# A third Strassen product taken as seven quarter-size products, with its right sums reloaded from DRAM

**Chip, cores, metric.** One core of a Trainium2 chip. The time is device microseconds of that core, given as the median of several executions.

## The reference, cut to what matters

```python
# attention between x (8 batches, 8 heads, 512 tokens, 64) and state (32 rows), both ways;
# concatenated tokens: 8 * (512 + 32), width 512
h = x @ w_in                                # 512 -> 2048
g = h * (1.0 / (1.0 + np.exp(-1.702 * h)))
return (g @ w_out).astype(np.float32)       # 2048 -> 512
```

The products with `w_in` are called up products here, those with `w_out` down products. All matmuls are fp32. TensorE does the matmuls and writes them to banks of the PSUM memory; VectorE does the sums. The batches go one after the other; then come the summary rows of all batches together ("sr" in the names).

## The kernel before

The product with `w_out` of batches 1 to 7 is one level of Strassen's scheme in Winograd's form: seven products P1 to P7 of halves. The weight is cut into B11, B21, B22, with the sums T1, T2, T3, T4 kept for all batches; the activations are cut into A11 to A22. Two of the seven, P6 (with T2) and P7 (with T3), are themselves done as seven products of quarters, by the function below. It needs sums of the left operand (made on VectorE in each batch) and of the right one (kept: `low2`, `low3`).

```python
def strassen_low(left, right, bank, R, at):
    b11, t3, b21, b22, t1, t2, t4 = right
    a11, a12, a21, a22, s1, s2, s4 = left
    p, u2, u3 = (pu[:, i] for i in range(3))
    o = [v[:, :P] for v in bank]                # three PSUM banks, used in turn
    ...
    product(o[0], a11, b11)                     # each product: 4 matmuls of 128 columns
    nc.scalar.copy(p, o[0])
    at(1)                                       # at(i): other work hooked in here
    product(o[1], s2, t2)
    add(u2, o[1], p)
    at(2)
    product(o[2], a12, b21)
    add(c11, o[2], p)
    at(3)
    product(o[0], a21, t3)
    add(u3, o[0], u2)
    at(4)
    product(o[1], s1, t1)                       # the bank of the second product again
    add(c22, o[1], u3)
    add(c12, o[1], u2)
    ...                                         # a22 t4, then s4 b22
```

A whole product is 2 x 8 matmuls of 256 columns. The end of a batch, in the order in which it is issued:

```python
    # P1, P2, P5 whole, P6 as seven small ones with T2, then:
    ...                                          # left sums for P7, eight VectorE operations
    for u in range(NU // 2, NU):
        s4(u)                                    # A12 made ready for P3
    tt(t01, bank(0), k2)
    hook("P6")
    product(bank(2), A_of(1, 1), T4, "P4")       # whole
    strassen_low(..., low_banks(), k3, ...)      # P7 with T3
    tt(k3, k3, k2)
    ...                                          # two outputs
    product(bank(3), A_of(0, 1), B22, "P3")      # whole
    tt(o01, bank(3), t01)
```

The hooks carry the attention and the up-product sums of the next batch; in batch 7 they carry the sums for the summary rows instead. In these traces VectorE's operations and TensorE's matmuls stand in the order in which the kernel issues them, so what is hooked in ahead of a sum delays that sum. The up products of the next batch follow directly.

Of the kernel before, what the change touches and what calls it, by code (L numbers as in the profile page):

```python
# [10 lines left out]
FP32 = mybir.dt.float32  # L11
# [3 lines left out]
ALU = mybir.AluOpType  # L15
# [5 lines left out]
def kernel(  # L21
# [30 lines left out]
    nc = tc.nc  # L52
# [27 lines left out]
    mpool = ctx.enter_context(tc.tile_pool(name="mpool", bufs=4))  # L80
    gpool = ctx.enter_context(tc.tile_pool(name="gpool", bufs=1))
    opool = ctx.enter_context(tc.tile_pool(name="opool", bufs=1))
    psA = ctx.enter_context(tc.tile_pool(name="psA", bufs=2, space=bass.MemoryType.PSUM))
    psH = ctx.enter_context(tc.tile_pool(name="psH", bufs=2, space=bass.MemoryType.PSUM))
    psO = ctx.enter_context(tc.tile_pool(name="psO", bufs=1, space=bass.MemoryType.PSUM))
# [495 lines left out]
    T3 = w_out[:, :HF, HN:]  # L581
    low2, low3 = ([low[:, 3 * i + k].rearrange("p (f n) -> p f n", f=QF) for k in range(3)] for i in range(2))

    def halves_of(t):

        return [t[:, QF * i : QF * (i + 1), P * k : P * (k + 1)] for i in range(2) for k in range(2)]

    def low_sums(t, rooms):

        b11, b12, b21, b22 = halves_of(t)  # L590
        t1, t2, t4 = rooms
        return [(T_of, v) for v in ((t1, b12, b11), (t2, b22, t1), (t4, b21, t2))]
# [40 lines left out]
        add(c12, o[0], c12)  # L633
        at(7)

    def strassen_two(key, dst, hooks):

        B11, B21, B22 = w_out[:, :HF, :HN], w_out[:, HF:, :HN], w_out[:, HF:, HN:]
        g = [G[key, u] for u in range(HF)]
        half = S // 2  # L640

        def A_of(i, k):
            return [quarters(key, (HF * k + f) // 2, S)[i][:, f % 2] for f in range(HF)]

        def hook(name):
            for fn, args in hooks.get(name, ()):
                fn(*args)

        def bank(i):
            return bank_o[i].rearrange("p (r n) -> p r n", r=2)  # L650

        def product(ps, lhs, rhs, name):
            for r in range(2):
                for f in range(HF):
                    nc.tensor.matmul(  # L655
                        ps[:, r], lhs[f][:, P * r : P * (r + 1)], rhs[:, f],
                        start=(r == 0 and f == 0), stop=(f == HF - 1), skip_group_check=True,
                    )
                hook(name + "ab"[r])

        def tt(out, x0, x1, op=ALU.add):
            nc.vector.tensor_tensor(out=out, in0=x0, in1=x1, op=op)

        def room(i):
            return later[:, i].rearrange("p (r n) -> p r n", r=2)

        def out(i, k, src):
            nc.sync.dma_start(dst(slice(2 * i, 2 * i + 2), slice(HN * k, HN * (k + 1))), src)

        def low_banks():  # L670
            h = [psH.tile([P, FC], FP32, tag="h", name=f"low_{key}") for _ in range(2)]
            return [bank_o[1], *h]


        q1, q2, q4 = (g[i][:, :, :half].rearrange("p k (h t) -> p k h t", h=2) for i in range(3))
        v1, v2, v4 = (later[:, 1 + i].rearrange("p (f t) -> p f t", f=QF) for i in range(3))
        k1 = g[3][:, :, :half]
        k2, k3, t01, o10, o01 = (room(i) for i in (0, 4, 5, 6, 7))
        z11, z12, z21, z22 = ([S2[:, QF * k + f, P * i : P * (i + 1)] for f in range(QF)] for i in range(2) for k in range(2))

        def whole(i, k):
            return S2[:, QF * k : QF * (k + 1), P * i : P * (i + 1)].rearrange("p (k h) t -> p k h t", h=2)

        def blocks(q):
            return [q[:, f // 2, f % 2] for f in range(QF)]

        product(bank(0), A_of(0, 0), B11, "P1")
        nc.scalar.copy(k1, bank(0))
        tt(q1, whole(1, 0), whole(1, 1))
        tt(q2, q1, whole(0, 0), ALU.subtract)  # L690
        tt(q4, whole(0, 1), q2, ALU.subtract)
        product(bank(1), A_of(0, 1), B21, "P2")
        osb = opool.tile([P, 2, HN], FP32, tag="osb", name=f"osb_{key}_00")
        tt(osb, bank(1), k1)
        out(0, 0, osb)

        def s4(u):
            a12 = quarters(key, NU + u, S)[0]
            tt(a12, a12, S2[:, 2 * u : 2 * u + 2, :half], ALU.subtract)

        for u in range(NU // 2):
            s4(u)
        tt(whole(1, 0), whole(0, 0), whole(1, 0), ALU.subtract)
        hook("P2")
        product(bank(0), [S1[:, f, :half] for f in range(HF)], T1, "P5")
        b11, t3, b21, b22 = halves_of(T2)
        strassen_low(
            (z11, z12, z21, z22, blocks(q1), blocks(q2), blocks(q4)), (b11, t3, b21, b22, *low2),
            low_banks(), k2, lambda i: hook(f"P6.{i}"),
        )  # L710
        tt(k2, k2, k1)

        def y(u, i):
            return g[u][:, :, half + P * i : half + P * (i + 1)]

        for u in range(NU // 2):
            w = slice(2 * u, 2 * u + 2)
            tt(v1[:, w], y(u, 1), y(2 + u, 1))
            tt(v2[:, w], v1[:, w], y(u, 0), ALU.subtract)
            tt(y(u, 1), y(u, 0), y(u, 1), ALU.subtract)  # L720
            tt(v4[:, w], y(2 + u, 0), v2[:, w], ALU.subtract)
        for u in range(NU // 2, NU):
            s4(u)
        tt(t01, bank(0), k2)
        hook("P6")
        product(bank(2), A_of(1, 1), T4, "P4")
        b11, t3, b21, b22 = halves_of(T3)

        def yl(k, i):
            return [y(2 * k + f // 2, i)[:, f % 2] for f in range(QF)]  # L730

        def vl(v):
            return [v[:, f] for f in range(QF)]

        strassen_low(
            (yl(0, 0), yl(1, 0), yl(0, 1), yl(1, 1), vl(v1), vl(v2), vl(v4)), (b11, t3, b21, b22, *low3),
            low_banks(), k3, lambda i: hook(f"P7.{i}"),
        )
        tt(k3, k3, k2)
        osb = opool.tile([P, 2, HN], FP32, tag="osb", name=f"osb_{key}_11")  # L740
        tt(osb, bank(0), k3)
        out(1, 1, osb)
        tt(o10, bank(2), k3)
        out(1, 0, o10)
        hook("P7")
        product(bank(3), A_of(0, 1), B22, "P3")
        tt(o01, bank(3), t01)
        out(0, 1, o01)
        free.extend(g)

    def hooks_next(b):

        h = {}

        def at(name, fn, *args):
            h.setdefault(name, []).append((fn, args))

        at("P1a", att_state, b)
        at("P1a", att_xT, b, 0)
        at("P1b", att_xT, b, 1)  # L760
        at("P1b", att_xT, b, 2)
        at("P1b", att_xT, b, 3, True)
        at("P2a", att_scores, b)
        at("P2a", att_M, b, 0)
        at("P2a", att_M, b, 1, True)
        at("P2a", att_blocks, b)
        at("P2a", att_s_max, b)
        at("P2a", att_s_exp, b)
        for g in range(NG):
            at("P2a", x_max, b, g)  # L770
            at("P2a", x_sub, b, g)
        at("P2a", x_exp, b)
        at("P2", att_s_norm, b)
        for name, fn, *args in (
            ("P6.1", x_sum, 0), ("P6.2", x_sum, 1), ("P6.3", x_inverse), ("P6.4", x_scale, 0), ("P6.6", x_scale, 1),
        ):
            at(name, fn, b, *args)
        for g in range(NG):
            at("P6", att_eT, b, g)
            at("P6", x_back, b, g)  # L780
        at("P4a", att_sread, b)
        at("P4a", att_M, b, 3, True)
        at("P4a", att_M, b, 2)
        steps = up_sums(b)
        for name, n in (("P4b", 5), ("P7.1", 2), ("P7.2", 1), ("P7.3", 1), ("P7.4", 1), ("P7.6", 1), ("P7", 1), ("P3a", 3)):
            for fn, args in steps[:n]:
                at(name, fn, *args)
            steps = steps[n:]
        assert not steps
        at("P3a", att_srT, b)  # L790
        return h


# [283 lines left out]
    def out_of(b):  # L1077
        return lambda r, n: out_x[b, r, :, n].rearrange("r q n -> q r n")

    for b in range(1, B):  # L1080
# [7 lines left out]
        if b + 1 < B:  # L1088
            hooks = hooks_next(b + 1)
        else:  # L1090

            steps, left, right = sr_sums()
            hooks = {"P3a": steps[9:] + [(low_third, (T2,)), (low_third, (T3,))]}
            for k, name in enumerate(("P1b", "P2a", "P2", "P5a", "P5b", "P6", "P4a", "P4b", "P7")):
                hooks[name] = [steps[k]]
        for name, first in ahead.items():
            hooks[name] = first + hooks.get(name, [])
        strassen_two(b, out_of(b), hooks)
        if b + 2 < B:
            load_state(b + 2)  # L1100
            load_x(b + 2)
# [35 lines left out]
```

## Time and profile before

| | before |
|---|---|
| time, median of 3 | 739.59 us (739.44 to 740.14) |
| TensorE busy | 98% |
| VectorE busy | 69% |
| a batch of the steady part | 80.1 us |
| whole product; seven small ones | 6.91 us; 6.25 us |

Read it from TensorE's list of waits and not from its busy share. The list says that outside the start nothing makes TensorE wait (the last wait is at 95.45 us, before the Strassen batches), so from there on the time is TensorE's instruction count times the spacing of its instructions. The prediction shows these lines.

### The profile page before, as it was taken

The page shows a single profiled execution, that of the slowest core. Times are in us where ns is not written, and L with a number is a line of the kernel's source. Part 1 is how long each engine was busy: PE and PEld are TensorE (multiplying, and loading weights), DVE is VectorE, ACT ScalarE, POOL GpSimd, SP SyncE. Part 2 cuts the span into 40 slices and gives each one's busy share as a digit, 9 for nine tenths or more (in the row PEclk, how much of TensorE's full clock was granted, in tenths as well). Part 3 has the DMA queues.
Part 4 walks back from the last instruction along what each step waited for, and adds up shares of the span by engine and source line. Part 5 has one row for each costly group of instructions (what it writes and reads, how often), then busy time and mean ns, then how long its engine had stood idle before and what let it go on. Part 6 is the DMA issues. An engine that isn't in the chain of part 4 may idle for free.

```text
span 737.6 us, 11080 instructions
## 1 busy us (share of the span) xinstructions
PE 724.4 (98%) x4613; PEld 566.4 (77%) x4615; DVE 509.7 (69%) x982; ACT 232.3 (31%) x424; POOL 0.8 (0%) x8
## 2 busy tenths in 40 slices
PE   7999999999999999999999999999999999999996
PEld 3333444478888789879888888878987988899995
DVE  6997999739756875677747675687566774767340
ACT  4786411033134411432144312441143214300210
POOL 0000000000000000000000000000000000000000
PEclk9999999999999999999999999999999999999999
DMA  9821244010040001300030004000130000000000
GB/s 233 343 91 53 94 157 126 0 58 15 1 104 1 16 1 49 56 1 16 29 76 1 15 2 104 1 15 1 46 59 1 15 27 18 1 15 29 16 1 28
DMA packets 48770, 35.31 MB, mean 48 GB/s; under 512 B 36432, under 2 KB 44112, under 8 KB 48720
## 3 DMA queue, kind: packets, MB, share of 16 engines
q1 hardware_dynamic: 48720, 34.61, 16.1%
q8 instruction: 36, 0.59, 0.3%
q14 instruction: 14, 0.11, 0.1%
HBM read 25.69 MB, written 8.91 MB: 47 GB/s over the span
## 4 chain that ended last, share of the span: by engine, by line
PE 95%; ACT 2%; DMA 2%; SPq 0%; DVE 0%; issue 0%; DVEq 0%; ACTq 0%
PE o L655 33%; PE o L900 16%; PE o L489 8%; PE low L607 7%; PE h L471 7%; PE upx L900 6%; PE o L607 5%; PE M L302 4%; PE o L532 2%; PE xT L281 2%; PE o L302 1%; PE sr L451 1%; PE warm L122 1%; PE upx_sr L900 1%; DMA out_dram<-osb_sr 1%; PE eT L440 1%
## 5 line engine op out<-in xcount | busy, mean ns | idle before, releaser
L655 PE MATMUL o<-w_out,g 128*128 128x256 f32 x672 | 151.8, 380 | 0.0
L910 DVE TENSOR_TENSOR g<-o,g 128x512 f32<-128x512 f32 (+1 forms) x140 | 88.1, 651 | 88.4 <-PE o L900 87.4
L655 PEld LDWEIGHTS o<-w_out,g 128*128 128x128 f32 x672 | 125.2, 190 | 21.7 <-issue 5.5
L907 ACT ACTIVATE g<-g 128x512 f32<-128x512 f32 (+1 forms) x84 | 49.8, 599 | 100.5 <-DVE g L910 100.5
L655 PE MATMUL o<-sums,g 128*128 128x256 f32 x224 | 51.1, 382 | 0.0
L655 PE MATMUL o<-sums,later 128*128 128x256 f32 x224 | 49.5, 379 | 0.0
L655 PEld LDWEIGHTS o<-sums,g 128*128 128x128 f32 x224 | 41.5, 190 | 10.1 <-issue 5.0
L900 PE MATMUL upx<-aT,M 128*128 128x256 f32 x192 | 49.3, 379 | 0.0
L900 PE MATMUL o<-ta,M 128*128 128x256 f32 x192 | 49.3, 379 | 0.0
L900 PE MATMUL o<-ta,ms 128*128 128x256 f32 x192 | 48.3, 379 | 0.0
L655 PEld LDWEIGHTS o<-sums,later 128*128 128x128 f32 x224 | 42.6, 190 | 5.8
L431 ACT COPY M<-M 128x512 f32<-128x512 f32 x64 | 33.2, 597 | 37.7 <-PE M L302 37.7
L900 PEld LDWEIGHTS o<-ta,ms 128*128 128x128 f32 x192 | 36.5, 190 | 5.0
L900 PEld LDWEIGHTS upx<-aT,M 128*128 128x128 f32 x192 | 36.5, 190 | 5.0
L900 PEld LDWEIGHTS o<-ta,M 128*128 128x128 f32 x192 | 36.5, 190 | 5.0
L610 DVE TENSOR_TENSOR pu<-low,pu 128x128 f32<-128x128 f32 x14 | 4.1, 291 | 43.8 <-PE low L607 43.8
L302 PE MATMUL M<-w_in,stT 64*32 64x512 f32 x512 | 32.7, 594 | 0.2 <-ACT eT L441 0.2
L512 DVE TENSOR_TENSOR later<-g,g 128x512 f32<-128x512 f32 (+1 forms) x32 | 20.8, 650 | 17.4 <-ACT g L474 17.4
L471 PE MATMUL h<-low,M 128*128 128x512 f32 x64 | 29.7, 600 | 1.5 <-DVE low L383 1.5
L471 PE MATMUL h<-aT,M 128*128 128x512 f32 x64 | 28.7, 599 | 1.4 <-ACT M L431 1.4
L614 ACT COPY pu<-o 128x128 f32<-128x128 f32 x14 | 3.7, 265 | 80.0 <-PE o L607 60.0
L489 PE MATMUL o<-w_out,g 128*128 128x512 f32 x64 | 28.7, 594 | 0.0
(176 smaller groups left out, 1123.5 us busy)
## 6 DMA issues: line engine op xcount, KB each, us to landing
later<-in_moe_w_out_dram SPq DMA_DIRECT2D x16, 512.0 KB
xn<-in_x_dram SPq DMA_DIRECT2D x28, 256.0 KB
w_out<-in_moe_w_in_dram SPq DMA_DIRECT2D x12, 512.0 KB
out_dram<-osb SPq DMA_DIRECT2D x18, 256.0 KB
out_dram<-later SPq DMA_DIRECT2D x14, 256.0 KB
later<-in_moe_w_in_dram SPq DMA_DIRECT2D x4, 512.0 KB
sums<-in_x_dram SPq DMA_DIRECT2D x4, 256.0 KB
stn<-in_state_dram SPq DMA_DIRECT2D x16, 32.0 KB
```

The costliest lines, as they stand in the source:

```text
L281: nc.tensor.transpose(ps[:, c], x_heads(b, c, j), ident)
L302: nc.tensor.matmul(ps[g][st], A[b]["stT"][rows, st], rhs(rows, j), start=True, stop=True)
L431: nc.scalar.copy(m[:, g], ps[g])
L471: nc.tensor.matmul(hps, lhs[i], rhs[i], start=(i == 0), stop=(i == n - 1))
L489: nc.tensor.matmul(ops, G[key, f // 2][:, f % 2, P * r : P * (r + 1)], w_out[:, f], start=(f == 0), stop=(f == NF - 1))
L512: nc.vector.tensor_tensor(out=s1, in0=a21, in1=a22, op=ALU.add)
L532: nc.tensor.matmul(ps[:, r], lhs[f][:, P * r : P * (r + 1)], rhs[:, f], start=(first and r == 0 and f == 0), stop=(f == HF - 1), skip_grou ...
L607: nc.tensor.matmul(ps, lhs[f], rhs[:, f], start=(f == 0), stop=(f == QF - 1))
L655: nc.tensor.matmul(ps[:, r], lhs[f][:, P * r : P * (r + 1)], rhs[:, f], start=(r == 0 and f == 0), stop=(f == HF - 1), skip_group_check=True,)
L900: nc.tensor.matmul(ps[:, k], lhs[i][:, o : o + P], rhs[i], start=(first and k == 0 and i == 0), stop=(i == n - 1), skip_group_check=True,)
L907: nc.scalar.activation(out=dst, in_=src, func=AF.Gelu_apprx_sigmoid)
L910: nc.vector.tensor_tensor(out=dst, in0=ps, in1=x, op=ALU.add)
```

## The change

The intent is to save one small product's worth of TensorE work per batch in a third place, P4 = A22 T4. The right sums of T4 (128 x 1536 fp32) get no room of their own on the chip. They are computed once, after batch 1, stored in DRAM, and in each of batches 2 to 7 loaded into the room of x after x was last read. For the transfer to have time, P3 goes where P4 was, and P4 goes last. Cut to its core:

```diff
+    kept4 = dram.tile([P, 3 * FC], FP32, name="low4")
+    def low4_load(a):
+        a["low4"] = low4_room()                 # the room of x
+        nc.sync.dma_start(a["low4"], kept4)
 ...
         hook("P2")
+        for u in range(NU // 2, NU):
+            s4(u)                               # was after P6
         product(bank(0), [S1...], T1, "P5")
 ...
         tt(t01, bank(0), k2)
         hook("P6")
-        product(bank(2), A_of(1, 1), T4, "P4")
+        if a4 is not None:                      # batches 2 to 7
+            left4 = sums(NU, (q1, q2, q4))      # eight VectorE operations
+        product(bank(3), A_of(0, 1), B22, "P3")
-        strassen_low((yl...), ..., low_banks(), k3, ...)
+        o, h0, h1 = low_banks()
+        strassen_low(left3, ..., [h0, h1, o], k3, ...)
 ...
+            strassen_low(left4, (..., *low4_parts(a4["low4"])), [o, h1, h0], k1, at)
-        product(bank(3), A_of(0, 1), B22, "P3")
 ...
+        if b == 1:
+            t = low4_room()
+            for fn, args in low_sums(T4, low4_parts(t)):
+                fn(*args)                       # three VectorE operations
+            nc.sync.dma_start(kept4, t)
+            low_third(T4)                       # a fourth
```

`low_third` replaces a quarter of T4 in place by a difference, and the same call undoes it later. The hooks of the last batch change as well: the sums of the summary rows move with the products that they hang on, and the restoring of T2, T3, T4 is spread over P3 and P4.

More of the change, by code (lines that the diff above doesn't have):

```diff
@@ L82 @@
     opool = ctx.enter_context(tc.tile_pool(name="opool", bufs=1))
+    dram = ctx.enter_context(tc.tile_pool(name="dram", bufs=1, space=bass.MemoryType.DRAM))
     psA = ctx.enter_context(tc.tile_pool(name="psA", bufs=2, space=bass.MemoryType.PSUM))
@@ L582, with low4_room, low4_parts @@
     low2, low3 = ([low[:, 3 * i + k].rearrange("p (f n) -> p f n", f=QF) for k in range(3)] for i in range(2))
+    kept4 = dram.tile([P, 3 * FC], FP32, name="low4")
+    def low4_room():
+        t = xpool.tile([P, SCH, H, D], FP32, tag="xn", name="low4")
+        return t.rearrange("p c h d -> p (c h d)")[:, : 3 * FC]
+    def low4_parts(t):
+        return [t[:, FC * k : FC * (k + 1)].rearrange("p (f n) -> p f n", f=QF) for k in range(3)]
+    def low4_load(a):
+        a["low4"] = low4_room()
+        nc.sync.dma_start(a["low4"], kept4)
     def halves_of(t):
@@ L634, in strassen_low, with strassen_two @@
         at(7)
-    def strassen_two(key, dst, hooks):
+    def strassen_two(key, dst, hooks, a4):
         B11, B21, B22 = w_out[:, :HF, :HN], w_out[:, HF:, :HN], w_out[:, HF:, HN:]
@@ L670, in low_banks @@
         def low_banks():
-            h = [psH.tile([P, FC], FP32, tag="h", name=f"low_{key}") for _ in range(2)]
-            return [bank_o[1], *h]
+            return [bank_o[1], *(psH.tile([P, FC], FP32, tag="h", name=f"low_{key}") for _ in range(2))]
         q1, q2, q4 = (g[i][:, :, :half].rearrange("p k (h t) -> p k h t", h=2) for i in range(3))
-        v1, v2, v4 = (later[:, 1 + i].rearrange("p (f t) -> p f t", f=QF) for i in range(3))
+        v1, v2, v4 = (later[:, 1 + i].rearrange("p (k h t) -> p k h t", k=2, h=2) for i in range(3))
         k1 = g[3][:, :, :half]
@@ L704, in strassen_two @@
         hook("P2")
+        for u in range(NU // 2, NU):
+            s4(u)
+        hook("S4")
         product(bank(0), [S1[:, f, :half] for f in range(HF)], T1, "P5")
@@ L711, in strassen_two, with sums, y, parts @@
         tt(k2, k2, k1)
-        def y(u, i):
-            return g[u][:, :, half + P * i : half + P * (i + 1)]
-        for u in range(NU // 2):
-            w = slice(2 * u, 2 * u + 2)
-            tt(v1[:, w], y(u, 1), y(2 + u, 1))
-            tt(v2[:, w], v1[:, w], y(u, 0), ALU.subtract)
-            tt(y(u, 1), y(u, 0), y(u, 1), ALU.subtract)
-            tt(v4[:, w], y(2 + u, 0), v2[:, w], ALU.subtract)
-        for u in range(NU // 2, NU):
-            s4(u)
+        def sums(u0, rooms):
+            def y(u, i):
+                return g[u0 + u][:, :, half + P * i : half + P * (i + 1)]
+            for u in range(NU // 2):
+                r1, r2, r4 = (v[:, u] for v in rooms)
+                tt(r1, y(u, 1), y(2 + u, 1))
+                tt(r2, r1, y(u, 0), ALU.subtract)
+                tt(y(u, 1), y(u, 0), y(u, 1), ALU.subtract)
+                tt(r4, y(2 + u, 0), r2, ALU.subtract)
+            def parts(k, i):
+                return [y(2 * k + f // 2, i)[:, f % 2] for f in range(QF)]
+            return parts(0, 0), parts(1, 0), parts(0, 1), parts(1, 1), *(blocks(v) for v in rooms)
@@ L724, in strassen_two @@
+        left3 = sums(0, (v1, v2, v4))
         tt(t01, bank(0), k2)
         hook("P6")
-        product(bank(2), A_of(1, 1), T4, "P4")
+        if a4 is not None:
+            left4 = sums(NU, (q1, q2, q4))
+        product(bank(3), A_of(0, 1), B22, "P3")
         b11, t3, b21, b22 = halves_of(T3)
-        def yl(k, i):
-            return [y(2 * k + f // 2, i)[:, f % 2] for f in range(QF)]
-        def vl(v):
-            return [v[:, f] for f in range(QF)]
-        strassen_low(
-            (yl(0, 0), yl(1, 0), yl(0, 1), yl(1, 1), vl(v1), vl(v2), vl(v4)), (b11, t3, b21, b22, *low3),
-            low_banks(), k3, lambda i: hook(f"P7.{i}"),
-        )
@@ L739, in strassen_two @@
-        tt(k3, k3, k2)
-        osb = opool.tile([P, 2, HN], FP32, tag="osb", name=f"osb_{key}_11")
-        tt(osb, bank(0), k3)
-        out(1, 1, osb)
-        tt(o10, bank(2), k3)
+        o, h0, h1 = low_banks()
+        strassen_low(left3, (b11, t3, b21, b22, *low3), [h0, h1, o], k3, lambda i: hook(f"P7.{i}"))
+        hook("P7")
+        osb = opool.tile([P, 2, HN], FP32, tag="osb", name=f"osb_{key}_11")
+        then = [
+            lambda: tt(k3, k3, k2),
+            lambda: tt(osb, bank(0), k3),
+            lambda: out(1, 1, osb),
+            lambda: tt(o01, bank(3), t01),
+            lambda: out(0, 1, o01),
+        ]
@@ new lines, in strassen_two, with at @@
+        if a4 is not None:
+            turn = {1: then[:1], 2: then[1:3], 3: then[3:]}
+            def at(i):
+                for fn in turn.get(i, ()):
+                    fn()
+                hook(f"P4.{i}")
+            b11, t3, b21, b22 = halves_of(T4)
+            o, h0, h1 = low_banks()
+            strassen_low(left4, (b11, t3, b21, b22, *low4_parts(a4["low4"])), [o, h1, h0], k1, at)
+            p4 = k1
+        else:
+            for fn in then:
+                fn()
+            product(bank(2), A_of(1, 1), T4, "P4")
+            for i in range(1, 8):
+                hook(f"P4.{i}")
+            p4 = bank(2)
@@ L744, in strassen_two @@
+        tt(o10, p4, k3)
         out(1, 0, o10)
-        hook("P7")
-        product(bank(3), A_of(0, 1), B22, "P3")
-        tt(o01, bank(3), t01)
-        out(0, 1, o01)
         free.extend(g)
@@ L780, in hooks_next @@
             at("P6", x_back, b, g)
-        at("P4a", att_sread, b)
-        at("P4a", att_M, b, 3, True)
-        at("P4a", att_M, b, 2)
+        at("P3a", att_sread, b)
+        at("P3a", att_M, b, 3, True)
+        at("P3a", att_M, b, 2)
         steps = up_sums(b)
-        for name, n in (("P4b", 5), ("P7.1", 2), ("P7.2", 1), ("P7.3", 1), ("P7.4", 1), ("P7.6", 1), ("P7", 1), ("P3a", 3)):
+        for name, n in (("P3a", 7), ("P7.1", 1), ("P7.2", 1), ("P7.3", 1), ("P7.4", 1), ("P7.6", 1), ("P4.4", 2), ("P4.6", 1)):
             for fn, args in steps[:n]:
@@ L789, in hooks_next @@
         assert not steps
-        at("P3a", att_srT, b)
+        at("P3b", att_srT, b)
         return h
@@ L1092 @@
             steps, left, right = sr_sums()
-            hooks = {"P3a": steps[9:] + [(low_third, (T2,)), (low_third, (T3,))]}
-            for k, name in enumerate(("P1b", "P2a", "P2", "P5a", "P5b", "P6", "P4a", "P4b", "P7")):
-                hooks[name] = [steps[k]]
+            hooks = {
+                name: [steps[k]]
+                for k, name in enumerate(("P1b", "P2a", "P2", "P5a", "P5b", "P6", "P3a", "P3b", "P7.1", "P7.2", "P7.3", "P7.4"))
+            }
+            hooks["P3b"].append((low_third, (T2,)))
+            hooks["P4.1"] = [(low_third, (T3,))]
+            hooks["P4.7"] = [(low_third, (T4,))]
         for name, first in ahead.items():
             hooks[name] = first + hooks.get(name, [])
-        strassen_two(b, out_of(b), hooks)
+        a4 = None
+        if b > 1:
+            a4 = {}
+            hooks["P3a"] = hooks.get("P3a", [])
+            k = 3 if b + 1 < B else 0
+            hooks["P3a"].insert(k, (low4_load, (a4,)))
+        strassen_two(b, out_of(b), hooks, a4)
+        if b == 1:
[4 more added lines that the diff above has]
+            low_third(T4)
         if b + 2 < B:
```

## The prediction

> **What bounds the kernel now.** I read the page first: its busy table, then who waited for whom on TensorE, then single stretches of one batch.
>
> ```profile
> PE 724.4 (98%) x4613; PEld 566.4 (77%) x4615; DVE 509.7 (69%) x982; ACT 232.3 (31%) x424; POOL 0.8 (0%) x8
> ```
>
> TensorE is busy for 98% of the span. Busy alone could hide stalls, so the next view is TensorE's list of waits (which group waited for which; us in total, times, longest):
>
> ```profile
> PE h L471 <- DVE low L383: 1.5, 1, 1.5
> PE h L471 <- ACT M L431: 1.4, 2, 0.8
> PE srT L461 <- ACT eT L441: 0.3, 1, 0.3
> ```
>
> Nothing in it is long, and nothing belongs to the down products of batches 1 to 7 (the 256-wide groups of line 655 and the 128-wide ones of line 607). So there the time is the number of matmuls times their start-to-start spacing: a matmul removed is time removed, and any wait put in front of one is time added. VectorE, at 69%, has idle time on average; what counts is whether it is idle where its results are awaited.
>
> The rate comes from the busy time by stretch, in batch 3 (stretch; its length, then busy time and instructions of PE, PEld, DVE, ACT, POOL; clock; DMA share, GB/s). The two stretches run from the first matmul of one product to the first of the next: a whole quarter product (16 matmuls in the code, 32 instructions), then the seven small products (28 in the code, 56 instructions).
>
> ```profile
> 333.63:340.54 6.91, 6.91 (x34) 6.08 (x33) 4.94 (x12) 1.51 (x3) 0.00 (x0) 1.00 0.11 38
> 340.54:346.79 6.25, 6.25 (x58) 6.25 (x57) 3.63 (x11) 0.27 (x1) 0.00 (x0) 1.00 0.01 3
> ```
>
> A whole product takes 6.91 us (216 ns an instruction), seven small ones 6.25 us (111.6 ns). The clock is 1.00 in both.
>
> **What the Trainium skill says.** "TensorE: Matmul & The Clock Gate", Back-to-back issue gap, gives N/2.4 + 2.5 ns for a warm matmul: 55.8 at 128 columns, 109.2 at 256. Twice that is 111.7 and 218; the trace has 111.6 and 216, so each instruction here behaves as two passes (the code's fp32 matmul shows as two instructions; "FP8 and Floating Point Precision", TensorE Precision Notes, gives true FP32 four passes, which fits). Halving the width thus costs 51.7%, not 50%, and seven of eight becomes 6.25/6.91 = 90.4%, not 87.5%. "VectorE: DVE Perf Modes", section The TRN2 errata, gives (N+151)/0.96 ns for an fp32 tensor_tensor: 291 ns at 128, 424 at 256, 691 at 512; the trace has 0.29, 0.42 and 0.68 to 0.69 us. Start to start they are closer in the trace: 0.60 us at 512 where the second doesn't need the first, 0.71 where it does.
>
> **The change, part by part.**
>
> (1) *TensorE work.* In batches 2 to 7 the product A22 T4 becomes seven small ones: 6.91 − 6.25 = 0.66 us less each, 6 × 0.66 = **−3.96 us**. Batch 1 keeps the whole product. Nothing else changes on TensorE; P3 takes P4's place between P6 and P7, with the same 32 instructions.
>
> (2) *VectorE work in batches 2 to 6.* Added: the left sums of A22, eight 128x256 operations, by the eight for A21 in the trace 2.93 us (347.92 to 350.86), and seven 128x128 adds of 0.29. Two 128x512 subtractions (1.20 us) move from after P6 to before P5, where VectorE now idles 3.85 us before its first P6 add. What limits is P7: its fifth product reuses the bank of the second and waits for that one's add. In the kernel before VectorE was early there:
>
> ```profile
> 355.51 0.69 DVE L799 TENSOR_TENSOR ms<-M 128x512 f32<-128x512 f32 x1
> 359.73 0.29 DVE L610 TENSOR_TENSOR pu<-low,pu 128x128 f32<-128x128 f32 x1 [3.53 <-PE low L607]
> ```
>
> It had 3.53 us of idle. The change puts 2.93 − 1.20 = 1.73 more ahead of that add, and one state sum (0.60) comes one place sooner: 3.53 − 2.33 = 1.2 us of idle remain. In the new small products each step of 0.893 us carries one add (0.2 to 0.3) and at most one 128x512 operation (0.6): it fits, as P7 with the same load does now. The next batch's first up product takes a bank that I work out to be read 0.3 to 0.4 us before it is wanted. Cost on the path: **0**.
>
> (3) *Batch 7.* Here the sums of the last block are hooked in: 128x1024 operations at 1.13 us start to start. Before, VectorE was already just in time:
>
> ```profile
> 670.53 1.22 DVE L863 TENSOR_TENSOR ws<-w_in,ws 128x1024 f32<-128x1024 f32 x1
> 671.66 0.28 DVE L610 TENSOR_TENSOR pu<-low,pu 128x128 f32<-128x128 f32 x1
> ```
>
> No bracket on the second line means no idle before it. The order of VectorE in the changed kernel after P6 (whose last add is at 662.59, then from 662.91) is: one 128x512 (0.61), eight 128x256 (2.93), one 128x512 (0.60), a 128x1024 (1.13), eight 128x256 (2.93), two 128x1024 (2.26), the restoring of T2 (0.60), a 128x256 (0.34), then P7's awaited add: 662.91 + 11.40 = 674.31, done at 674.60. The trace has P7 start at 669.29, so its fifth product would start at 669.29 + 4 × 0.893 = 672.86. TensorE waits from there to about 674.65: **+1.8 us**. After it the adds keep up.
>
> (4) *Batch 1 to 2.* The right sums of T4 are made once, after batch 1: three 128x512 (two dependent) and the restoring one. They stand before the first add of batch 2's up products. Before:
>
> ```profile
> 210.95 0.69 DVE L662 TENSOR_TENSOR later<-o,later 128x512 f32<-128x512 f32 x1 [2.88 <-PE o L655]
> 212.75 0.69 DVE L910 TENSOR_TENSOR g<-o,g 128x512 f32<-128x512 f32 x1 [1.11 <-PE o L900]
> 214.20 1.03 PE L900 MATMUL o<-ta,M 128*128 128x256 f32 x4
> ```
>
> The last line accumulates into the bank which the add at 212.75 reads. With the four put in, that add starts at 210.95 + 0.61 + 0.71 + 0.71 + 0.61 + 0.60 = 214.19 and ends at 214.88: **+0.7 us** for TensorE, once.
>
> (5) *DMA.* Each of batches 2 to 7 reloads 128 x 1536 fp32 = 786 KB into x's room, after the transposed read of x in P3's first half (in batch 3's times at about 352.3). It is wanted at the second small product of P4, about 364.8: 12.5 us. "DMA: Bandwidth & Descriptors", Bandwidth, measures 6.15 us for 1 MB (another issuing path); the trace's x load of 1.05 MB in 256-byte pieces was through by about 380.5 after issue at 373.55, 7 us, so the larger rows of this load should take 4 to 6 by my estimate. Hidden. The next x load can then begin only after P4's use of the room, but it was last in the queue anyway (issued after both outputs, at 373.55) and is wanted at 398.7: hidden. After batch 1 it also waits for the sums to be written out, by my estimate 8 us; it has 18 to spare. Cost **0**.
>
> Sum: 739.59 − 3.96 + 1.8 + 0.7 = **738.1 us**.
>
> **Rivals.** *No wait appears:* if both VectorE backlogs are hidden, the time is 739.59 − 3.96 = 735.6. For it speaks 31% of idle VectorE; against it, the two places have no idle time left in the trace, and the waits are fixed by the banks. *The small products stall in each batch:* P4 follows P7 directly, so fourteen small products run on three banks with full-width operations between the adds. Half a microsecond in each of 5 batches gives 740.6. Against it: P7 carries such a load now without a wait of TensorE, and 1.2 us of idle remain. *The reload comes late:* if each load took over 12.5 us, TensorE would stand 1 us or more in six batches, over 744. Against it: the queue moves 131 to 238 GB/s for outputs and x in this trace, and in P3 and P7 the DMA share is 0.01 or less.
>
> **Range and chances.** The saving is arithmetic on one rate and nearly certain. The two waits are read to some 0.5 us each. Low end: one of them mostly absent, 736.2. High end: small stalls of 0.25 us in each of five batches, 739.4. Two per cent is 14.8 us, and the most that the change can save is 4; a loss of 14.8 needs a transfer missed in every batch. Faster 1%, same 98%, slower 1%.
>
> **What would show it.** (1) 336 more 128-wide and 192 fewer 256-wide down instructions, at the same spacing; one batch of 2 to 6 shortens from 80.1 us (from 242.54 to 322.64, the transposes of x in two successive batches) to about 79.4. (3) and (4) A new wait on VectorE's add in TensorE's list: about 1.8 us in P7 of the last batch, about 0.7 us in batch 2's first up products. (5) No wait of TensorE for the reload. I am wrong if the batches of 2 to 6 show waits in P7 or P4, if the last batch shows none, or if TensorE waits for x or for the reload.

## The result

The changed kernel takes 738.23 us (738.22 to 738.32, 4 runs). In the same set the kernel before took 739.52 us (739.29 to 740.14). The ratio is 0.9982, with an interval of 0.9964 to 0.9999. Differences can be read here because the fast runs of one kernel lie within 0.1 to 0.9 us of each other, most within 0.3. Predicted were 738.1 us, within 736.2 to 739.4.

The busy table of the page after the change (engine, busy us, share, instructions):

```profile
PE 720.9 (98%) x4757; PEld 567.4 (77%) x4759; DVE 539.4 (73%) x1077; ACT 233.8 (32%) x430; POOL 0.8 (0%) x8
```

TensorE has 144 more instructions (336 narrow ones more, 192 wide ones fewer) and is busy 3.5 us less. VectorE is busy 30 us more. The share of TensorE did not move, so this line tells nothing of the gain.

P7 and the new P4 of batch 3, busy time by stretch (columns as in the prediction):

```profile
357.93:364.18 6.25, 6.25 (x58) 6.25 (x57) 4.43 (x11) 0.53 (x2) 0.00 (x0) 1.00 0.00 0
364.18:370.44 6.26, 6.26 (x59) 6.26 (x57) 4.97 (x13) 0.27 (x1) 0.00 (x0) 1.00 0.27 86
```

Both sets of small products run at the rate of the old ones. VectorE fills 71% and 79% of them and TensorE waits in neither. A steady batch is now 79.45 us (the first transposes of x in successive batches lie at 239.29 and, two batches later, 398.18).

Who waited for whom, TensorE, after (us in total, times, longest):

```profile
PE low L622 <- DVE pu L625: 1.6, 1, 1.6
...
PE o L938 <- DVE g L948: 0.6, 1, 0.6
```

Two lines are new, each one single wait. The first is in the last batch, before P7's fifth product. TensorE and VectorE there, in order of time (start, us, engine, line, operation; in brackets the idle time before it):

```profile
669.50 1.06 PE L622 MATMUL low<-w_out,g 128*128 128x128 f32 x8
672.20 1.16 PE L622 MATMUL low<-low,later 128*128 128x128 f32 x8 [1.63 <-DVE pu L625]
673.19 1.06 PE L622 MATMUL o<-low,g 128*128 128x128 f32 x8
```

```profile
668.65 1.22 DVE L901 TENSOR_TENSOR w_in<-w_in,w_in 128x1024 f32<-128x1024 f32 x1
669.78 1.22 DVE L901 TENSOR_TENSOR ws<-w_in,ws 128x1024 f32<-128x1024 f32 x1
670.92 0.68 DVE L1080 TENSOR_TENSOR sums<-sums 128x512 f32<-128x512 f32 x1
671.52 0.42 DVE L901 TENSOR_TENSOR ta_sr<-srT 128x256 f32<-128x256 f32 x1
671.86 0.28 DVE L625 TENSOR_TENSOR pu<-low,pu 128x128 f32<-128x128 f32 x1
```

The fourth small product starts at 669.50, so the fifth was due at 669.50 + 0.89 = 670.40. It started at 672.20, just after VectorE's add. Look also at its length: from 672.20 to the next product are 0.99 us instead of 0.89. So this wait cost TensorE the delay and then 0.10 us more: 1.80 + 0.10 = 1.90 us. The records of the weight loads (PEld) show what differs there. Elsewhere the first weight load of a small product starts 0.10 us before its first matmul, while the matmuls before it still run (669.40 for 669.50, 673.08 for 673.19); after the wait the two start together (672.19 and 672.20). That this is the cause of the 0.10 us is read from the trace; no run tests it.

The second wait is after batch 1:

```profile
213.56 0.68 DVE L1080 TENSOR_TENSOR sums<-sums 128x512 f32<-128x512 f32 x1
214.16 0.68 DVE L948 TENSOR_TENSOR g<-o,g 128x512 f32<-128x512 f32 x1
```

```profile
213.29 1.03 PE L938 MATMUL upx<-aT,M 128*128 128x256 f32 x4
214.90 1.13 PE L938 MATMUL o<-ta,M 128*128 128x256 f32 x4 [0.58 <-DVE g L948]
215.87 1.03 PE L938 MATMUL upx<-aT,M 128*128 128x256 f32 x4
```

Due at 213.29 + 0.86 = 214.15, started at 214.90, and again 0.10 to 0.11 us longer: 0.86 us in all.

The sum closes. From the first product of batch 1 to the last product of the summary rows the two traces take 728.19 − 154.82 = 573.37 us and 726.97 − 154.78 = 572.19 us, 1.18 less. The small products save 6 x 0.66 = 3.96 (in batch 3, where P4 takes 6.26, 0.01 less), the waits cost 1.90 + 0.86 = 2.76, and the difference is 1.20.

The reload of batch 3 is issued at 352.52. Its data show in the last two columns (DMA share, GB/s) of these stretches:

```profile
353.00:355.00 2.00, 2.00 (x34) 0.83 (x12) 1.93 (x6) 1.44 (x3) 0.00 (x0) 1.00 0.70 199
355.00:357.00 2.00, 2.00 (x11) 1.75 (x10) 1.97 (x7) 0.62 (x2) 0.00 (x0) 1.00 0.49 203
357.00:359.00 2.00, 2.00 (x16) 1.85 (x15) 1.55 (x3) 0.27 (x1) 0.00 (x0) 1.00 0.00 0
```

It is through by 357, within 4.5 us of its issue, and is wanted at 365.08. Finer stretches put its end at 356.3, 3.8 us after the issue.

### The profile page after: what moved, and what is told of

Read it like the earlier page. It is cut to its first block, busy times and chain, and to the rows that moved or that the text cites. A ratio compares the mean times of both kernels' runs of the same rounds, so it can differ in the third digit from the quotient of the medians.

```text
span 736.3 us, 11509 instructions
## 1 busy us (share of the span) xinstructions
PE 720.9 (98%) x4757; PEld 567.4 (77%) x4759; DVE 539.4 (73%) x1077; ACT 233.8 (32%) x430; POOL 0.8 (0%) x8
## 4 chain that ended last, share of the span: by engine, by line
PE 93%; DVE 2%; ACT 2%; DMA 2%; issue 0%; SPq 0%; DVEq 0%; ACTq 0%
PE o L670 27%; PE o L938 16%; PE low L622 10%; PE o L490 8%; PE h L472 7%; PE o L622 6%; PE upx L938 5%; PE M L303 4%; PE o L533 2%; PE xT L282 2%; PE o L303 1%; PE sr L452 1%; PE warm L123 1%; PE upx_sr L938 1%; DMA out_dram<-osb_sr 1%; PE eT L441 1%
## 5 line engine op out<-in xcount | busy, mean ns | idle before, releaser
L622 PE MATMUL low<-low,g 128*128 128x128 f32 x256 | 32.8, 275 | 0.0
L622 PEld LDWEIGHTS low<-low,g 128*128 128x128 f32 x256 | 30.7, 192 | 0.0
L625 DVE TENSOR_TENSOR pu<-low,pu 128x128 f32<-128x128 f32 x27 | 7.8, 290 | 29.1 <-PE low L622 29.1
```

The source lines that it names most:

```text
L622: nc.tensor.matmul(ps, lhs[f], rhs[:, f], start=(f == 0), stop=(f == QF - 1))
```

## The experiments

My theory: the saving is that of the matmul count, and two single waits for VectorE give most of it back. The rivals: the waits are symptoms and their time would come back elsewhere; the new order or the reload costs something; the steady batches are nearly as tight as the last. The runs have five rounds each (four times for e9), with the kernel before on the same chip (739.36 to 739.38 us there). The changed kernel was not run again in these sets: where a run is compared with it, its 738.23 us is from the set of the result, in which the kernel before took 739.52. All gave correct results.

| run | median us | ratio to before | 95% interval |
|---|---|---|---|
| e1 last batch's hooks moved | 736.39 | 0.9960 | 0.9948 to 0.9973 |
| e2 T4's right sums sooner | 737.41 | 0.9973 | 0.9961 to 0.9986 |
| e3 both | 735.61 | 0.9950 | 0.9937 to 0.9962 |
| e4 order alone | 739.27 | 0.9999 | 0.9986 to 1.0013 |
| e5 reload twice | 738.13 | 0.9983 | 0.9969 to 0.9997 |
| e6 last batch whole | 736.92 | 0.9969 | 0.9957 to 0.9982 |
| e7 old bank order | 742.13 | 1.0037 | 1.0023 to 1.0051 |
| e8 three operations put in | 738.26 | 0.9985 | 0.9971 to 0.9999 |
| e9 six operations put in | 747.32 | 1.0107 | 1.0093 to 1.0120 |

**e1, the last batch.** Two sums of the summary rows and the restoring of T2 go behind the awaited add. (P3a and P3b are the hooks after the two halves of P3, P7.6 is the sixth hook inside P7.)

```diff
-  ... "P5b", "P6", "P3a", "P3b", "P7.1", "P7.2", "P7.3", "P7.4"
+  ... "P5b", "P6", "P7.6", "P4.4", "P7.1", "P7.2", "P7.3", "P7.4"
-            hooks["P3b"].append((low_third, (T2,)))
+            hooks["P4.6"] = [(low_third, (T2,))]
```

> Theory (the 1.8 us wait in P7 of the last batch comes from VectorE work put ahead of the awaited add): two 128x1024 sums and the restoring of T2 are put 2.86 us of VectorE time later, so the add is ready in time and the time falls by 1.8 us, to 736.4 us; no wait of 'low' on 'pu' is left in TensorE's list. Rival (the wait is only where an unavoidable lag shows): the wait comes back at the next small products or at the summary rows' first products, and the time stays within 0.5 us of 738.2.

Measured 736.39 us, and the wait is gone from the list. In the trace of e1, VectorE's add and the fifth small product:

```profile
669.12 0.28 DVE L625 TENSOR_TENSOR pu<-low,pu 128x128 f32<-128x128 f32 x1
```

```profile
670.53 1.06 PE L622 MATMUL low<-low,later 128*128 128x128 f32 x8
```

The add is over 1.1 us before the bank is wanted. From P7's first matmul to the summary rows' first are 12.50 us (666.96 to 679.46), against 14.40 in the changed kernel (666.83 to 681.23): exactly the 1.90 us of the wait. The work that was moved did not make TensorE wait in a later place.

**e2, after batch 1.** The three right sums go into VectorE's idle time during batch 1's P4.

```diff
+        if b == 1:
+            def keep4():
+                t = low4_room()
+                for fn, args in low_sums(T4, low4_parts(t)):
+                    fn(*args)
+                nc.sync.dma_start(kept4, t)
+            hooks["P4.7"] = hooks.get("P4.7", []) + [(keep4, ())]
 ...
         if b == 1:
-            t = low4_room()
-            ...                                 # the sums and the store
             low_third(T4)
```

> Theory (the 0.6 us wait in batch 2's first up products comes from the four T4 operations ahead of the first add): the three right sums are put into the 3.4 us in which VectorE idles in batch 1's P4, only the restoring one stays; the wait goes and the time falls by 0.7 us, to 737.5 us. Rival: the first add is late for another reason (the activation, the state loads), and the time stays at 738.2 us.

Measured 737.41 us; this wait, too, is gone, and the one of the last batch is still there.

**e3, both edits.**

> Theory: the two waits are independent, both go, and the full saving of the matmuls stands: 739.5 - 3.96 = 735.6 us. Rival (something else of the change costs, or the small products save less): above 736.2 us.

Measured 735.61 us: the whole saving stands and the two waits were independent. Neither is in the list any more. From the first product of batch 1 to the last of the summary rows its trace takes 724.31 − 154.87 = 569.44 us, against 573.37 before. The interval lies below that of the changed kernel, and its slowest run (736.04) is below the fastest of the changed kernel (738.22), so this version beats both kernels.

**e4, the order alone.** The changed order with P4 whole in all batches, no reload and no sums of T4 (`a4` stays None in every batch).

> The order of the changed kernel with A22 T4 whole in all batches: no reload, no sums of T4. Theory (the order alone is worth nothing, as TensorE has the same matmuls and no waits): 739.5 us, within 0.3 of before. Rival (putting P3 sooner itself gains or loses): differs from before by over 0.7 us.

Measured 739.27 us, a ratio of 0.9999. The order neither gains nor loses by itself. It is there to give the transfer time; whether the change would also work without it was not tested.

**e5, the reload done twice.**

```diff
-        nc.sync.dma_start(a["low4"], kept4)
+        for _ in range(2):
+            nc.sync.dma_start(a["low4"], kept4)
```

> Each reload of T4's sums is done twice into the same room, one after the other. In the changed kernel one reload is issued at 352.5 and has moved its data by about 357; it is wanted at 365.1. Theory (the reload is hidden with some 8 us to spare): two end at about 362, the time stays 738.2 us within 0.3. Rival (reloads disturb other transfers or are near the path): over 0.7 us longer.

Measured 738.13 us. The second load is seen in the trace of e5 (columns as above):

```profile
359.00:361.00 2.00, 2.00 (x21) 2.00 (x20) 0.88 (x3) 0.27 (x1) 0.00 (x0) 1.00 0.68 280
361.00:363.00 2.00, 2.00 (x21) 2.00 (x20) 1.99 (x7) 0.00 (x0) 0.00 (x0) 1.00 0.00 0
```

It ends by about 361, still 4 us early. The reload is hidden, and so is twice the reload.

**e6, the last batch kept whole.** P4 of batch 7 is a whole product again (T4 restored after batch 6).

```diff
-        if b > 1:
+        if 1 < b < B - 1:
             a4 = {}
 ...
+        if b == B - 2:
+            low_third(T4)
```

> The last batch keeps A22 T4 as a whole product; batches 2 to 6 have the seven. Theory (in the last batch the change saves 0.66 us of matmuls and costs a wait of 1.8 us, which comes from VectorE's eight left sums of A22 among other work): the wait goes, the matmuls come back: 738.2 - 1.8 + 0.66 = 737.1 us. Rival (the wait has nothing to do with the left sums, but with the hooks of the last sums): the wait stays and the time is 738.9 us.

Measured 736.92 us: doing less of the change is faster by 1.3 us than doing all of it. In the last batch the new product saved 0.66 us and cost 1.90. Of what e6 takes out of the last batch (the left sums, the adds of the small products, the reload), only the eight left sums stand ahead of the awaited add. So they are needed for the wait: without them, the same hooks ahead of that add do no harm. With e1, which keeps the left sums and moves the hooks, it shows that either one alone fits and that the sum of the two does not.

**e7, the old order of the banks.**

```diff
-        strassen_low(left3, ..., [h0, h1, o], k3, ...)
+        strassen_low(left3, ..., [o, h0, h1], k3, ...)
-            strassen_low(left4, ..., [o, h1, h0], k1, at)
+            strassen_low(left4, ..., [o, h0, h1], k1, at)
```

> P7 and P4 both take the banks in the order of the kernel before, so that P4's first product writes the bank of P7's last one, which VectorE reads only then. Theory (TensorE must wait for that add: it ended 0.5 us after P7's last product in the changed kernel): 0.55 us in each of batches 2 to 7, 738.2 + 3.3 = 741.5 us, and a new wait of 'o' on VectorE's 'later', six times. Rival (the order of the banks does not matter, the reader is done in time): 738.2 us.

Measured 742.13 us. The list of waits and the first product of P4 in batch 3, in the trace of e7:

```profile
PE o L622 <- DVE later L625: 2.3, 6, 0.4
```

```profile
364.20 1.06 PE L622 MATMUL o<-w_out,later 128*128 128x128 f32 x8
365.64 1.16 PE L622 MATMUL o<-sums,g 128*128 128x128 f32 x8 [0.38 <-DVE later L625]
366.63 1.06 PE L622 MATMUL low<-low,g 128*128 128x128 f32 x8
```

P4's first product was due at 364.20 + 0.89 = 365.09 and started 0.55 us late, as expected; it then took 0.10 us longer. 6 x 0.65 = 3.9 us, which is 742.13 − 738.23. The expectation had left out the 0.10. Of the idle time alone the list shows 0.38 each, less than the loss: the listed idle of a wait is not its whole cost. The two different rotations that the change carries are together worth as much as all that it saves; one of them alone was not tried.

**e8 and e9, how much slack the steady batches have.** Three or six 128x512 operations without effect (each the maximum of a tile with itself, in a tile that is written afterwards) are put ahead of the awaited add of P7, in batches 2 to 6.

```diff
+            if i == 1 and a4 is not None and key < B - 1:
+                for _ in range(3):              # e9: 6
+                    tt(k3, k3, k3, ALU.max)
```

> Three idle operations (128x512, each needing the one before, 0.71 us start to start, 2.1 us in all) are put on VectorE ahead of the add that P7's fifth product awaits, in batches 2 to 6. In the changed kernel VectorE is idle 1.41 us there, and the add ends 1.2 us before it is wanted, 2.6 us of slack in all. Theory: the 2.1 us fit, the time stays 738.2 us within 0.4. Rival (these batches are just as tight as the last one, and the lag is carried into P4): 0.5 us or more in each of the five, over 740.7 us.

Measured 738.26 us: 2.1 us more on VectorE in each of five batches cost nothing.

> Six of the same operations, 4.3 us, against 2.6 us of slack. Theory (a wait of 4.3 - 2.6 = 1.6 us or so before P7's fifth product in each of batches 2 to 6, and nothing else): 738.2 + 5 x 1.6 = 746.3 us, and five more waits of 'low' on 'pu' of 1.4 to 1.7 us. Rival (the lag is also carried into P4 and the up products): over 748 us; rival (TensorE makes it up later): under 744 us.

Measured 747.32 us, 9.1 more than the changed kernel, 1.8 in each of the five batches. In its trace of batch 3 the fifth product starts 1.59 us late (365.06, due at 363.47), takes 0.10 longer, and P4's first product loses another 0.12, a small lag carried over. So the steady batches have about 2.6 us of slack: 4.23 us were put in (360.49 to 364.72), and 1.59 of them came out as delay. The expectation of 746.3 us had left out what follows the wait, 5 x 0.22 = 1.1 us.

## Why the prediction was right

**What bounds it.** Right. Batches of 2 to 6 without a wait shortened as the matmul count says (79.45 us against 79.4 foretold).

**(1) The saving.** Right: e3, where the waits are gone, is at 735.61 us, and the step's sum gives 735.6. From the first product of batch 1 to the last of the summary rows the trace of e3 is 3.93 us shorter than that of the kernel before, against 3.96 foretold.

**(2) No cost in batches 2 to 6.** Right. The remaining idle ahead of P7's add was put at 1.2 us. After the change it reads:

```profile
357.89 0.69 DVE L837 TENSOR_TENSOR ms<-ms,M 128x512 f32<-128x512 f32 x1
359.99 0.29 DVE L625 TENSOR_TENSOR pu<-low,pu 128x128 f32<-128x128 f32 x1 [1.41 <-PE low L622]
```

That is 1.41. Idle was only a part of the slack of 2.6 us, as e8 and e9 show. The rest is that the add itself could come 1.2 us later: it ends at 360.28, and its bank is wanted only at the fifth product, at 361.50.

**(3) The last batch.** The mechanism, the place and the delay (1.8 us) were right; e1 and e6 confirm the cause from two sides. The term was mis-sized by the 0.10 us by which the first product after the wait is longer: 1.90.

**(4) After batch 1.** Right in mechanism and place, confirmed by e2. The term was 0.7; it measured 0.86, of which 0.11 is again the longer first group after the wait.

**(5) The reload.** Right that it is hidden: e5 shows room for a second. It took 3.8 us, just under the 4 to 6 estimated. One reading is misnamed: the DMA share of "0.01 or less in P3 and P7" is that of the stretch in which P4 stood before and P3 stands now (0.01 from 347.66 to 357.68); in the old place of P3, after P7, it was 0.22.

**Rivals.** That no wait appears was wrong for the change as given, but it is what e3 makes true. Stalls of the small products in each batch did not come; e7 shows that they would have come with the banks in their old order. The late reload fell.

**What is left open.** Whether the new product can also go into batch 1 was not tried. The spread of 0.1 to 0.2 us between sets of runs is as large as the rest that the accounting leaves.

## What to carry to other kernels

When the bounding engine has no gaps, work taken from it is time saved, and the whole question is where the helpers, now busier, will make it wait. Their average idle does not answer that (VectorE was idle for 31% of the span here); follow the helper's queue, operation by operation, to the one result that is awaited, above all in the first and last pass of a loop, where other work hangs on the same hooks. Here two short waits took 70% of the gain, and moving a few operations, behind the awaited one (e1) or into idle time before it (e2), gave it all back.

## What the Trainium skill lacked or had wrong

- "TensorE: Matmul & The Clock Gate", Back-to-back issue gap, has no row for fp32. Here each matmul of the code is two instructions, each spaced 111.6 ns at 128 columns and 216 ns at 256, about twice what the formula there gives, which the section calls that of an isolated matmul.
- No page gives what a wait costs TensorE beyond the delay. In these runs the first group after a wait took 0.10 to 0.11 us longer (0.99 instead of 0.89 us, and 0.97 instead of 0.86).
- "VectorE: DVE Perf Modes", The TRN2 errata, gives the length of one operation (691 ns at 512, which the trace has). What counts in a queue is the start-to-start spacing, and no page has a figure for an operation that reads the result of the one before it: 0.71 us here at 128x512 in fp32, against 0.60 where the two are independent.
- "DMA: Bandwidth & Descriptors", Bandwidth, has no reload of this form. 786 KB in 128 rows of 6 KB took 3.8 us here from issue to the end of its traffic; over the two stretches of 2 us that hold it, it moved 199 and 203 GB/s.
